# Scores in three steps of 512 columns, first half of O after four of h, and the gate spread by PE, in a kernel of attention and a sentence-level expert layer

## The chip, the cores and the metric

The kernel runs on one core of one Trainium2 chip. The metric is device microseconds of one execution. Every run of an experiment was timed beside runs of the kernel before on the same chip. A run is called fast or slow by its state; only fast runs are compared here.

An engine is named as the profile names it: PE is TensorE, PEld its weight loads, DVE VectorE, ACT ScalarE, POOL GpSimd, SP SyncE. A "quarter" is half a batch's heads: there are 8 batches and 16 quarters, each with four heads of 64 columns over a sequence of 576. The texts on record count quarters in two ways: "the quarter after the fourth" has index 4, counted from 0.

## The reference, cut to what matters

```python
# q, k, v: (8 batches, 8 heads, 576, 64); f: (8, 8, 576), gates in (0.8, 1)
scores = q @ k.T / 8
cum    = cumsum(log(clip(f, 1e-4, 1)))
scores = where(causal, scores + cum[i] - cum[j], -1e9)
attn   = softmax(scores)
x      = (attn @ v), heads side by side            # (8, 576, 512)
# one expert per batch
e      = argmax(x.mean(axis=1) @ w_gate)           # 8 experts
gate   = softmax(x.mean(axis=1) @ w_gate)[e]
out    = gate * (relu(x @ w1[e]) @ w2[e])          # w1: 512x1024, w2: 1024x512
```

The decay is folded into the weights of V, so that the device computes an exp of the plain scores, a mask, and two products: with weighted V, and with the weights alone for the row sums.

## The kernel before

The program is not written as a sequence. It declares some 1,090 operations with durations, dependences, buffers and priorities, and a list scheduler (class `Order`) plans them on a model of the engines and of the DMA queues. The plan is made when the kernel is built; what it leaves is one fixed order of instructions for each engine. On the chip each engine takes its instructions in that order and waits where an operand is missing.

```python
# constants of the scheduler that matter here
FILL = 60.0            # until then PE is given filler matmuls where its plan is empty
PM0  = 12.0            # priority of the expert layers against attention
LAG  = 3               # K and Q of a quarter are loaded three quarters ahead
LOOK = {1: (0, 0, 0), 2: (0, 1, 2), 3: (1, 0, 2), 4: (1, 0, 2)}   # quarters loaded early
...
# Order.run, cut: the free engine takes the ready operation of the lowest priority number
if pick is not None and (best is None or pick.prio < best[1].prio):
    best = (e, pick)
if best is None and self.filler is not None and now < self.fill_until and busy["PE"] <= now + 1e-9:
    ...                                     # a filler matmul: still (zeros), 128x512
```

Scores of a quarter take four steps of 448, 448, 384 and 320 columns; each step writes two PSUM tiles of two banks (two heads each), and each tile has an exp of its own:

```python
PS_S = [psum.tile([P, 2, 512], fp32, name=f"ps_s{i}") for i in range(2)]
...
def expo(g, s, halves):
    e = E[od.slot(("e", g))][s]
    for n in halves:
        nc.scalar.activation(e[:, 2 * n:2 * n + 2, :],
                             PS_S[od.slot(("s", (g, s, n)))][:, :, 0:WIDTH[s]], AF.Exp, scale=0.125)
...
raws[g, 1].behind = raws[g, 1].behind if g in LOOK else [ld2] if g < 6 else [wvs[g - LAG][0]]
```

The first two quarters go by half steps (two heads at a time). After a batch's two quarters come its gate, the load of its expert's weights, 64 matmuls of h (128x288, sixteen units of four) and ten units of O (the output product), which are planned side by side with the attention of later quarters.

The softmax here doesn't subtract the row's maximum and nothing guards it: scores larger than these inputs give would overflow.

Of the kernel before, what the change touches and what calls it, by code (L numbers as in the profile page):

```python
# [11 lines left out]
P = 128  # L12
S = 576
# [11 lines left out]
STEPS = (((0, 0, 448, 0),),  # L25
         ((1, 128, 576, 0),),
         ((2, 256, 576, 0), (4, 512, 576, 320)),
         ((3, 384, 576, 0), (0, 448, 576, 192)))
WIDTH = (448, 448, 384, 320)

BLOCKS = ((0, 256, ((0, 0, 0, 256, 0), (1, 1, 128, 256, 0))),
          (256, 576, ((1, 1, 256, 576, 128), (0, 0, 256, 448, 256), (2, 2, 256, 576, 0),
                      (0, 3, 448, 576, 192), (3, 3, 384, 576, 0), (4, 2, 512, 576, 320))))

MAX_SPAN = 72.0

W_LOW, W_HIGH = 8.6e-17, 1.2e16
LN_SCALE = 2.0 ** -3
FILL = 60.0
# [5 lines left out]
PM0 = 12.0  # L45
LAG = 3
# [5 lines left out]
LOOK = {1: (0, 0, 0), 2: (0, 1, 2), 3: (1, 0, 2), 4: (1, 0, 2)}  # L52


class Op:
# [3 lines left out]
    def __init__(self, name, engines, us, fn, after=(), prio=0.0, takes=(), gives=(), lands=None, grain=None, runs=0, behind=()):  # L59
        self.name, self.us, self.fn, self.prio = name, us, fn, prio  # L60
        self.engines = engines if isinstance(engines, tuple) else (engines,)
        self.after, self.takes, self.gives, self.lands = list(after), takes, gives, lands
        self.end, self.grain, self.runs = None, grain, runs
        self.behind, self.issued = behind, None
        self.engine = None


class Order:
# [4 lines left out]
    def __init__(self, rings):  # L73
        self.free = {k: [(0.0, i) for i in range(n)] for k, n in rings.items()}
        self.held = {}
        self.turn = {k: [] for k in rings if k != "bank"}
        self.ops = []
        self.queues = {"SP": [], "ACT": [], "POOL": []}
        self.clock, self.last = 0.0, "full"
        self.filler, self.fill_until, self.spare = None, 0.0, 0  # L80
# [22 lines left out]
    def advance(self, now):  # L103


        while self.clock < now - 1e-9:
# [9 lines left out]
            for q in live:  # L116
                if q[0][1] < 1e-6:
                    op = q.pop(0)[3]
                    op.end = self.clock + 0.4
                    self.give(op)  # L120

# [17 lines left out]

    def run(self):  # L140
        left = list(self.ops)
        busy = dict.fromkeys(("PE", "ACT", "DVE", "POOL", "SP"), 0.0)
        now = 0.0
        busy["PE"] = 2.0
        while left:
# [5 lines left out]
            for e, until in busy.items():  # L151
# [4 lines left out]
                for op in left:  # L156
                    if e not in op.engines:
                        continue
                    ready = 0.0
                    for a in op.after:  # L160
                        if a.end is None:
                            ready = None
                            break
                        ready = max(ready, a.end + (0.0 if a.engine == e and a.lands is None else self.HOP))
                    for a in op.behind:
                        if a.issued is None:
                            ready = None
                        elif ready is not None:
                            ready = max(ready, a.issued)
                    if ready is None:  # L170
                        continue
# [13 lines left out]
            if best is None and self.filler is not None and now < self.fill_until and busy["PE"] <= now + 1e-9:  # L185
# [9 lines left out]
            if best is None:  # L195
                assert horizon is not None, (self.held, [o.name for o in left if all(a.end is not None for a in o.after)])
# [3 lines left out]
            op.engine = e  # L200
            for ring, key in op.takes:
# [4 lines left out]
                if ring in self.turn:  # L206
                    self.turn[ring].pop(0)
            if e == "PE" and self.mode(op) != self.last:
# [11 lines left out]
            left.remove(op)  # L220
# [5 lines left out]
def fast_path(ctx, tc, q, k, v, f, moe_w_gate, moe_w1, moe_w2, out, flag):  # L226
# [12 lines left out]
    PS_S = [psum.tile([P, 2, 512], fp32, name=f"ps_s{i}") for i in range(2)]  # L239
# [3 lines left out]
    KT = [const.tile([P, S], fp32, name=f"kt{i}") for i in range(RINGS["qt"])]  # L243
    VF = [const.tile([P, NCH, NH, D], fp32, name=f"vf{i}") for i in range(RINGS["vf"])]
    VB = [const.tile([P, NCH, 4, D], bf16, name=f"vb{i}") for i in range(RINGS["vb"])]
    E = [[const.tile([P, 4, WIDTH[s]], bf16, name=f"e{s}{i}") for s in range(4)] for i in range(RINGS["e"])]
# [13 lines left out]
    ROW = small("row", [1, P])  # L260
    seen_to = const.tile([P, 1], fp32, name="seen")[64:65, :]
# [5 lines left out]
    span = const.tile([NB * NH, 1], fp32, name="span")  # L267
    mxs = const.tile([1, NB * NH], fp32, name="mxs")
    mx8 = const.tile([1, 8], fp32, name="mx8f")
    WF = const.tile([P, NB, NCH, NH], fp32, name="WF")  # L270
    WB = const.tile([P, NB, NCH, NH], bf16, name="WB")
    wg = const.tile([P, 4, NE], fp32, name="wg")
    ident = const.tile([D, D], fp32, name="identf")
    still = const.tile([P, 512], bf16, name="still")

# [34 lines left out]
    def first(op):  # L310
        nc.scalar.preload_act_table_set("natural_log_exp_and_others")
        nc.sync.dma_start(F, f.rearrange("b h s -> (b h) s"))
        nc.vector.memset(still, 0.0)  # L313
        for t in VB:
            nc.vector.memset(t[0:64, 4, :, :], 0.0)
        nc.vector.memset(WF[0:64, :, 4, :], 0.0)

    loadf = od.add("F", "SP", 0.5, first, prio=-50, lands=0.5, grain=.1)
    idop = od.add("ident", "POOL", 0.8, lambda op: make_identity(nc, ident), prio=-1)
# [9 lines left out]
    last = [loadf]  # L329
    for b in range(NB):  # L330
        for c in range(10 if b < VQ else 5):
# [3 lines left out]
                                   takes=(("vf", b),) if c == 0 else (), lands=(1.4 if c5 < 4 else .7) / (2 if b < VQ else 1), grain=.022, runs=(64 if c5 < 4 else 32) // (2 if b < VQ else 1),  # L335
                                   behind=last if b < VQ else [loads_v[b, c - 1]] if c else [])
# [13 lines left out]
    def cum3(op):  # L350
        nc.vector.tensor_scalar_mul(mid, span, -0.5)
        nc.vector.tensor_tensor_scan(CUM, LOGF, LOGF, mid[:, 0:1], op0=ALU.add, op1=ALU.bypass)
# [13 lines left out]
    def cum6(op):  # L366
        pw = PS_W[od.slot(("bank", "cum"))]
        for w in (WF[:, :, 0:4, :], WF[64:P, :, 4, :]):
            nc.vector.tensor_scalar(w, w, W_LOW, W_HIGH, op0=ALU.max, op1=ALU.min)
        nc.vector.tensor_copy(WB.rearrange("p b c h -> p (b c h)"), WF.rearrange("p b c h -> p (b c h)"))  # L370
# [5 lines left out]
    c2 = od.add("cum2", "ACT", 0.68, cum2, after=[c1], prio=0.5)  # L376
    c3 = od.add("cum3", "DVE", 1.45, cum3, after=[c2], prio=2)
    c4 = od.add("cum4", "PE", 0.8, cum4, after=[c3, idop], prio=0, takes=(("bank", "cum"),))
    c5 = od.add("cum5", "ACT", .7, cum5, after=[c4], prio=0)
    c6 = od.add("cum6", "DVE", 0.9, cum6, after=[c5], prio=0, gives=(("bank", "cum"),))  # L380
# [3 lines left out]
    def to_t(g, j, lo=0, hi=4):  # L384
        raw = RAW[j][od.slot(("raw", g))][32 * lo:32 * hi].bitcast(fp32).rearrange("p (r w) -> p r w", w=32)
        dst = (QT, KT)[j][od.slot(("qt", g))][32 * lo:32 * hi].rearrange("p (t r) -> p r t", r=18)
        nc.vector.transpose(dst, raw)  # L387

    def banks_of(g, s, n):

        i = od.slot(("s", (g, s, n)))
        return [(2 * n + j, PS_S[i][:, j, :]) for j in range(2)]

    def step(g, s, halves):
        i = od.slot(("qt", g))
        kt, qt = KT[i].bitcast(bf16).rearrange("p (t r) -> p t r", r=2), QT[i].bitcast(bf16).rearrange("p (t r) -> p t r", r=2)
        for c, i0, i1, col in STEPS[s]:
            for r in range(2):
                for h, ps in [x for n in halves for x in banks_of(g, s, n)]:
                    nc.tensor.matmul(ps[:, col:col + i1 - i0], kt[32 * h:32 * h + 32, KLO[c]:KLO[c] + P, r],  # L400
                                     qt[32 * h:32 * h + 32, i0:i1, r], start=(r == 0), stop=(r == 1))

    def expo(g, s, halves):
        e = E[od.slot(("e", g))][s]
        for n in halves:
            nc.scalar.activation(e[:, 2 * n:2 * n + 2, :], PS_S[od.slot(("s", (g, s, n)))][:, :, 0:WIDTH[s]], AF.Exp, scale=0.125)  # L406

    def mask(g, s):
        e = E[od.slot(("e", g))][s]
        nc.gpsimd.affine_select(out=e[:, :, 0:128], in_=e[:, :, 0:128], pattern=[[0, 4], [1, 128]],  # L410
                                channel_multiplier=-1, base=0, compare_op=ALU.is_ge, fill=0.0)
        if s == 2:
            nc.gpsimd.affine_select(out=e[:, :, 320:384], in_=e[:, :, 320:384], pattern=[[0, 4], [1, 64]],
                                    channel_multiplier=-1, base=64, compare_op=ALU.is_ge, fill=0.0)

    def weigh(op, g, part):
# [8 lines left out]
        else:  # L425
            eng.tensor_tensor(vb[64:P, 4, :, :], vf[64:P, 4, h, :],
                                    WF[64:P, b, 4, h].unsqueeze(2).to_broadcast([64, 4, D]), op=ALU.mult)

    def pv(g, blk, what, lo_n=0, hi_n=6):
# [38 lines left out]
    last_s = []  # L468
    tk, steps, exps, masks, pvs, wvs = {}, {}, {}, {}, {}, {}
    for g in range(NQ):  # L470
        b, m = divmod(g, 2)
        p = 3.0 * g
        for n in (0, 1) if g == 0 else ():
            for j in (1, 0):
                tk[0, j, n] = od.add(f"T0{j}h{n}", "DVE", 1.15, lambda op, j=j, n=n: to_t(0, j, 2 * n, 2 * n + 2), after=[raws[0, j, n]] + ([tk[0, 1, n]] if j == 0 else []), prio=p + .1 * n,
                                     takes=(("qt", 0),) if j > n else (), gives=(("raw", 0),) if n > j else ())
        for j in (1, 0) if g else ():
            tk[g, j] = od.add(f"T{g}{j}", "DVE", 1.15, lambda op, g=g, j=j: to_t(g, j), after=[raws[g, j]] + ([tk[g, 1]] if j == 0 else []), prio=p,
                              takes=(("qt", g),) if j == 1 else (), gives=(("raw", g),) if j == 0 else ())
        if g == 0:  # L480
# [3 lines left out]
        for part in (0, 1, 2):  # L484
            wv.append(od.add(f"V{g}{part}", "POOL" if g > 1 or part == 1 and g == 0 else "DVE" if g == 0 else ("DVE", "POOL"), 1.1 if part < 2 else 0.7, lambda op, g=g, part=part: weigh(op, g, part), prio=p + 1.5,
# [3 lines left out]
        for s in range(4):  # L489
            steps[g, s], exps[g, s] = [], []  # L490
        turns = [(s, x) for x in cut for s in range(4)] if g == 0 and len(cut) > 1 else [(s, x) for s in range(4) for x in cut]
        for s, halves in turns:
            n = WIDTH[s]
# [365 lines left out]
```

## Time and profile before

| | kernel before |
|---|---|
| median of three runs | 249.45 us (249.1 to 251.54) |
| profiled run, span | 250.8 us |
| first h matmul, last matmul ends | 39.3 us, 244.4 us |
| PE idle between them (gaps of 0.15 us or more, summed from the trace) | 8.7 us |

The prediction shows the page's first lines, a table of stages and three lines of the start. One more view is needed later: the table of PE's waits (columns: the waiting engine with what it writes and its line, the engine that released it with what it had written, then us in total, times, longest us).

```profile
PE ps_s L400 <- ACT e L406: 2.8, 6, 1.0
PE ps_w L595 <- DVE xT L459: 1.9, 1, 1.9
PE ps_w L439 <- issue: 1.5, 2, 0.9
PE ps_w L595 <- DMA w1e<-in_moe_w_dram: 1.5, 2, 1.0
```

The reader is to see that no wait is large: scores wait 2.8 us for exps in 250 us, and weights cost 1.5 us, all at the first expert. "Issue" means that the profile shows no releaser; what stands behind it turns up below.

### The profile page before, as it was taken

The page shows a single profiled execution, that of the slowest core. Times are in us where ns is not written, and L with a number is a line of the kernel's source. Part 1 is how long each engine was busy: PE and PEld are TensorE (multiplying, and loading weights), DVE is VectorE, ACT ScalarE, POOL GpSimd, SP SyncE. Part 2 cuts the span into 40 slices and gives each one's busy share as a digit, 9 for nine tenths or more (in the row PEclk, how much of TensorE's full clock was granted, in tenths as well). Part 3 has the DMA queues.
Part 4 walks back from the last instruction along what each step waited for, and adds up shares of the span by engine and source line. Part 5 has one row for each costly group of instructions (what it writes and reads, how often), then busy time and mean ns, then how long its engine had stood idle before and what let it go on. Part 6 is the DMA issues. An engine that isn't in the chain of part 4 may idle for free.

```text
span 250.8 us, 8039 instructions
## 1 busy us (share of the span) xinstructions
PE 229.7 (92%) x3304; PEld 146.2 (58%) x3325; DVE 115.4 (46%) x305; ACT 177.2 (71%) x313; POOL 127.0 (51%) x197
## 2 busy tenths in 40 slices
PE   6799997999889999799999999899998999999990
PEld 2333734674366846567458755586586656957840
DVE  3892882667533941278136942694146342200000
ACT  3466846897799968849779874896488787855820
POOL 6046739971995546714992649363822872300000
PEclk9657999999999999979999999999999999999996
DMA  6996849999999999990999999999993598299032
GB/s 119 221 221 118 146 73 180 201 207 212 177 220 212 215 204 226 297 213 8 173 219 213 277 218 215 254 227 209 227 278 76 82 232 216 36 212 256 29 121 75
DMA packets 59946, 45.84 MB, mean 183 GB/s; under 512 B 40896, under 2 KB 43968, under 8 KB 59904
## 3 DMA queue, kind: packets, MB, share of 16 engines
q0 software_dynamic: 14848, 26.22, 59.1%
q1 hardware_dynamic: 32576, 15.90, 25.1%
q10 hardware_dynamic: 12480, 3.15, 6.1%
q8 instruction: 28, 0.46, 0.7%
q14 instruction: 14, 0.11, 0.1%
HBM read 62.03 MB, written 9.44 MB: 285 GB/s over the span
## 4 chain that ended last, share of the span: by engine, by line
PE 73%; DMA 7%; issue 6%; POOL 6%; ACT 3%; DVE 2%; POOLq 1%; ACTq 0%; DVEq 0%
PE ps_w L595 24%; PE ps_w L612 20%; PE ps_s L400 12%; PE ps_w L439 11%; PE ps_w L615 3%; PE ps_w L680 3%; DMA out_dram<-otile 3%; DMA w1e<-in_moe_w_dram 2%; ACT e L406 2%; DMA rawq<-in_q_dram 2%; POOL e L410 2%; POOL vb L423 1%; DVE qt L387 1%; POOL rawk L281 1%; PE ps_w L548 1%
## 5 line engine op out<-in xcount | busy, mean ns | idle before, releaser
L406 ACT ACTIVATE e<-ps_s 128x896 bf16<-128x896 f32 (+2 forms) x128 | 100.2, 834 | 28.7 <-PE ps_s L400 27.9
L410 POOL TENSOR_SCALAR_AFFINE_SELECT e<-e 128x512 bf16<-128x512 bf16 x64 | 41.7, 656 | 69.0 <-ACT e L406 68.4
L595 PE MATMUL ps_w<-xT,w1e 128*128 128x288 bf16 x512 | 71.0, 292 | 3.4 <-DVE xT L459 1.9
L595 PEld LDWEIGHTS <-w1e 128*128 128x128 bf16 x512 | 60.5, 139 | 11.5 <-issue 4.9
L612 PE MATMUL ps_w<-w2e,h1T 128*128 128x512 bf16 x239 | 57.5, 380 | 1.9 <-issue 1.4
L400 PE MATMUL ps_s<-qt,kt 32*128 32x448 bf16 (+4 forms) x768 | 42.1, 289 | 5.6 <-ACT e L406 2.8
L459 DVE SCALAR_TENSOR_TENSOR xT<-ps_w,lr 128x256 bf16<-128x256 f32 (+1 forms) x64 | 26.8, 455 | 37.1 <-ACT lr L449 30.6
L605 ACT ACTIVATE h1T<-ps_w,gate_b 128x288 bf16<-128x288 f32 x77 | 37.4, 499 | 4.9 <-PE ps_w L595 4.7
L612 PEld LDWEIGHTS <-h1T 128*128 128x128 bf16 x256 | 22.8, 98 | 28.5 <-issue 3.6
L603 DVE TENSOR_SCALAR h1T<-ps_w,gate_b 128x288 bf16<-128x288 f32 x51 | 25.3, 505 | 28.6 <-PE ps_w L595 28.2
L400 PEld LDWEIGHTS <-kt 32*128 32x128 bf16 x768 | 17.6, 95 | 27.5 <-issue 21.5
L439 PE MATMUL ps_w<-e,vb 128*32 128x320 bf16 (+4 forms) x1024 | 29.4, 251 | 1.8 <-issue 1.5
L423 POOL TENSOR_TENSOR vb<-vf,WF 128x512 bf16<-128x512 f32 x29 | 30.5, 1053 | 0.3
L387 DVE STREAM_TRANSPOSE kt<-rawk 128x576 f32<-128x576 f32 (+1 forms) x17 | 21.3, 1252 | 19.4 <-DMA rawk<-in_k_dram 16.3
L624 ACT COPY otile<-ps_w 128x512 f32<-128x512 f32 (+1 forms) x25 | 14.0, 560 | 21.9 <-PE ps_w L612 20.9
L439 PEld LDWEIGHTS <-vb 128*32 128x32 bf16 x1024 | 21.3, 97 | 7.0 <-issue 4.7
L387 DVE STREAM_TRANSPOSE qt<-rawq 128x576 f32<-128x576 f32 (+1 forms) x17 | 21.1, 1244 | 0.6 <-DMA rawq<-in_q_dram 0.5
L680 PE MATMUL ps_w<-still 128*128 128x512 bf16 x51 | 17.4, 472 | 2.1 <-DVE still L313 1.4
L622 DVE COPY otile<-ps_w 128x512 f32<-128x512 f32 (+1 forms) x15 | 9.0, 599 | 21.2 <-PE ps_w L612 19.8
L439 PE MATMUL ps_w<-e,WB 128*32 128x192 bf16 (+4 forms) x512 | 17.3, 253 | 0.1
L576 POOL DMA_DIRECT2D w1e<-in_moe_w_dram x14 | 10.2, 731 | 13.1 <-DVE h1T L603 11.4
L444 ACT ACTIVATE lr<-ps_w 128x256 f32<-128x256 f32 (+1 forms) x31 | 12.7, 411 | 4.8 <-PE ps_w L439 4.5
(55 smaller groups left out, 129.4 us busy)
## 6 DMA issues: line engine op xcount, KB each, us to landing
w2e<-in_moe_w_dram POOLq DMA_DIRECT2D x8, 1024.0 KB, 14.2
out_dram<-otile SPq DMA_DIRECT2D x32, 256.0 KB, 7.4
w1e<-in_moe_w_dram POOLq DMA_DIRECT2D x14, 512.0 KB, 7.6
rawk<-in_k_dram POOLq DMA_DIRECT2D x15, 288.0 KB, 7.2
rawq<-in_q_dram POOLq DMA_DIRECT2D x15, 288.0 KB, 8.7
vf<-in_v_dram SPq DMA_DIRECT2D x12, 256.0 KB, 9.3
vf<-in_v_dram ACTq DMA_DIRECT2D x12, 256.0 KB, 12.2
vf<-in_v_dram SPq DMA_DIRECT2D x22, 128.0 KB, 6.0
```

The costliest lines, as they stand in the source:

```text
L387: nc.vector.transpose(dst, raw)
L400: nc.tensor.matmul(ps[:, col:col + i1 - i0], kt[32 * h:32 * h + 32, KLO[c]:KLO[c] + P, r], qt[32 * h:32 * h + 32, i0:i1, r], start=(r == 0 ...
L406: nc.scalar.activation(e[:, 2 * n:2 * n + 2, :], PS_S[od.slot(("s", (g, s, n)))][:, :, 0:WIDTH[s]], AF.Exp, scale=0.125)
L410: nc.gpsimd.affine_select(out=e[:, :, 0:128], in_=e[:, :, 0:128], pattern=[[0, 4], [1, 128]], channel_multiplier=-1, base=0, compare_op=AL ...
L423: eng.tensor_tensor(vb[:, c, :, :], vf[:, c, h, :], WF[:, b, c, h].unsqueeze(3).to_broadcast([P, 2, 4, D]), op=ALU.mult)
L439: nc.tensor.matmul(ps[32 * h:32 * h + 32, lo - i0:hi - i0], lhs, e[s][:, h, col:col + hi - lo], start=(n == 0), stop=(n == len(parts) - 1) ...
L459: nc.vector.scalar_tensor_tensor(XT[od.slot(("x", b))][:, mm, i0:i1], ps[:, 0:i1 - i0], 1.0 if (g, blk) in ON_DVE else LN_SCALE, LR[od.slo ...
L595: nc.tensor.matmul(ps[:, 0:288], lhs, xT[:, m, 288 * half:288 * half + 288], start=(m == 0), stop=(m == 3))
L603: nc.vector.tensor_scalar(dst, ps[:, 0:288], g[:, 0:1], 0.0, op0=ALU.mult, op1=ALU.max)
L605: nc.scalar.activation(dst, ps[:, 0:288], AF.Relu, scale=g[:, 0:1])
L612: nc.tensor.matmul(ps, h[:, j, P * sb:P * sb + P], r, start=(j == 0), stop=(j == 7))
L680: od.filler = lambda i: nc.tensor.matmul(PS_W[i], still[:, 0:P], still[:, 0:512])
```

## The change

It repacks the causal scores of a quarter into three steps of 512 columns, so that a whole step of four heads fills one PSUM tile of four banks exactly and gets one exp of 128x2048. Two pieces of 64 columns share a place by a K that is padded with zeros. It also lets the first half of an O product start after four of the eight h blocks, spreads the gate value over partitions by a PE matmul instead of a DMA, moves some masks to DVE, replaces clamps, lets V loads start only after f has landed, drops the fillers of the first 28 us of the plan, corrects durations in the scheduler's model, and changes its load constants. Its core:

```diff
-STEPS = (((0, 0, 448, 0),),
-         ((1, 128, 576, 0),),
-         ((2, 256, 576, 0), (4, 512, 576, 320)),
-         ((3, 384, 576, 0), (0, 448, 576, 192)))
+STEPS = (((0, 0, 512, 0),),
+         ((1, 128, 576, 0), (0, 512, 576, 448)),
+         ((2, 256, 576, 0), (None, 384, 512, 320), (3, 448, 576, 384)))
...
-FILL = 60.0
+FILL = (28.0, 60.0)
-PM0 = 12.0
-LAG = 3
+PM0 = 11.0
+LAG = 2
-LOOK = {1: (0, 0, 0), 2: (0, 1, 2), 3: (1, 0, 2), 4: (1, 0, 2)}
+LOOK = {1: (0, 0, 0), 2: (0, 1, 2), 3: (1, 0, 2)}
...
-    PS_S = [psum.tile([P, 2, 512], fp32, name=f"ps_s{i}") for i in range(2)]
+    PS_S = psum.tile([P, 4, 512], fp32, name="ps_s")
...
     def expo(g, s, halves):
         e = E[od.slot(("e", g))][s]
-        for n in halves:
-            nc.scalar.activation(e[:, 2 * n:2 * n + 2, :], PS_S[...][:, :, 0:WIDTH[s]], AF.Exp, scale=0.125)
+        if len(halves) == 2:
+            nc.scalar.activation(e, PS_S, AF.Exp, scale=0.125)
+        else:
+            for lo, bank in banks_of(g, s, halves):
+                nc.scalar.activation(e[:, lo:lo + 2, :], PS_S[:, bank:bank + 2, :], AF.Exp, scale=0.125)
...
     def gate6(op, b):
-        nc.sync.dma_start(GATE[i], ROW[i])
+        nc.tensor.matmul(ps[:, 0:1], ROW[i], one)
...
-            om = od.add(f"O{b}{sb}a", ..., after=list(rel.values()) + outs[-1:] + [ld2], ...)
+            om = od.add(f"O{b}{sb}a", ..., after=[x for (j, _), x in rel.items() if j < 4] + outs[-1:] + [ld2], ...)
```

One thing about it is easily read past: because the order is made by the scheduler, every changed duration and constant draws a new order for all engines, over the whole 250 us.

## The prediction

> **What bounds the kernel now.** I read the page first: busy shares, then the forty slices, then the chain of waits.
>
> ```profile
> span 250.8 us, 8039 instructions
> PE 229.7 (92%) x3304; PEld 146.2 (58%) x3325; DVE 115.4 (46%) x305; ACT 177.2 (71%) x313; POOL 127.0 (51%) x197
> ...
> PEclk9657999999999999979999999999999999999996
> ...
> PE 73%; DMA 7%; issue 6%; POOL 6%; ACT 3%; DVE 2%; POOLq 1%; ACTq 0%; DVEq 0%
> ```
>
> PE is busy 92% of the time and carries 73% of the chain, so an engine other than PE matters only where PE waits for it or runs filler. The clock row shows half clock in the first slices. The table of stages (columns: stretch, length, busy us of each engine with instruction counts, clock, DMA share, GB/s) separates a start, a body and a tail:
>
> ```profile
> 7.80:21.40 13.60, 13.03 (x74) 4.54 (x74) 11.27 (x17) 6.97 (x10) 5.19 (x8) 0.50 1.04 194
> 21.40:43.80 22.40, 19.89 (x342) 10.89 (x337) 13.13 (x33) 15.67 (x26) 14.78 (x26) 1.00 0.83 135
> 43.80:213.00 169.20, 161.67 (x2663) 106.67 (x2678) 85.06 (x238) 132.58 (x234) 100.48 (x149) 0.99 1.01 204
> 213.00:244.50 31.50, 31.11 (x225) 22.64 (x225) 2.46 (x13) 19.33 (x40) 2.19 (x3) 1.00 0.58 129
> ```
>
> Up to 43.8 us PE looks busy, but much of it is filler on the tile `still`: 51 matmuls, 17.4 us. By starts and columns, useful columns there are worth only about 15 us at full clock. The body and tail are nearly solid. The timeline shows what filler does in the start:
>
> ```profile
> 15.13 1.24 DVE L387 STREAM_TRANSPOSE qt<-rawq 128x576 f32<-128x576 f32 x1
> ...
> 18.64 2.31 PE L680 MATMUL ps_w<-still 128*128 128x512 bf16 x5
> ...
> 20.88 0.82 PE L400 MATMUL ps_s<-qt,kt 32*128 32x448 bf16 x8
> ```
>
> Queries of the second quarter are ready at 16.37 us, yet its first scores start at 20.88: PE takes instructions in their fixed order, and five fillers at half clock stand ahead of them. The same happens at 12.73 (three fillers ahead of scores whose operands were ready at 11.82). The exps of that quarter end at 29.3, its last normalization at 32.3, the gate follows, the first expert weights are issued at 35.48, and the first h matmul starts at 39.31. From there PE is the bound until 244.5; a copy and a store take the last 6.3 us.
>
> **What the Trainium skill says.** "TensorE: Matmul & The Clock Gate", Part 1, gives a clock that is half when cold and full after about 3.4 us of sustained work. The trace agrees on the two values: 0.5 from 7.79 to 21.44 us, 1.0 after, and one dip of 3.41 us at 106.8. Its Part 3 says that matmuls in different row groups run concurrently, starting about 4 ns apart; here four heads' matmuls start 3 to 4 ns apart. "TensorEngine Tiling (Array Packing)", Key Properties, says that changing the tiling mode drains the engine. The trace agrees: a warm 512-column matmul is followed by the next after 216 ns, but by a row-tiled score after 312, so a change costs about 96 to 110 ns. "ScalarE: Activation LUTs", Step-by-step: what each stage is for, gives 0.833 ns per element for an activation; here 896 columns take 913 ns and 768 take 807, that is 0.83 per column.
>
> **The change part by part.**
>
> *Scores.* Columns per head and quarter: before 2×(448+448+384+320) = 3200; after 2×(512+512+320+128) plus four shared pieces of 64 = 3200 again. Score matmuls go from 768 to 896, those of attention times values from 1536 to 1728. These are small ones, four side by side: groups of four of 64 columns start some 20 to 27 ns after one another, 128 columns 46, 192 columns 72. Columns decide, so PE pays nearly nothing.
>
> *Exps.* Before, by shape: 55.2+24.4+20.9 = 100.5 us. After: 42 of 128×2048 at an estimated 0.913+1152×0.00083 = 1.87 us, and 12 of 128×1024 at 1.02: 91 us. ACT gets some 10 us back. It was at 71%, so this is mostly off the path, but 12 exps stand on the path in the start.
>
> *Mode changes.* The built order has 168 changes of PE mode before and 133 after; from the first h matmul on, 140 and 118. 22 × 0.1 = **2.2 us** on the path.
>
> *Fillers.* 55 fall to 10, all after the first 28 us of the scheduler's plan. Also, loads of V now wait until f has landed, so Q and K come first. I walk the start. Before, the first Q half lands at 6.71, slowed by V loads from 1.61 on; after, I expect about 5.3, and first scores at 7.0 instead of 8.04. DVE then does its transposes some 1.1 us earlier; clamps (0.52) and the flag (0.6) leave its front; the second quarter's Q is ready near 14.7 instead of 16.37. With no filler ahead, its scores run from about 16 to 23, still at half clock (a pair of 512-column half steps is 4×512/1.2 GHz = 1.7 us). Its exps then end at 23.5 to 24.5 instead of 29.3. Masks and values add 2.5, exps of the row sums and normalization 1.1: last normalization at about 28 instead of 32.3. A 1.25 us transpose of Q that now stands between the pooled sums and the top logit moves ahead. Weights issued at about 30.1 instead of 35.48, first h at about 33.9: **5.4 us** earlier, with the same work done (3.0 quarters of scores against 2.83, two of values in both).
>
> *Gate by PE.* The spread by DMA took 6.3 us to land in the median, but h matmuls do not read it; in batch 1 it lands at 69.2 and h starts at 73.7. Hidden: 0. The eight new matmuls cost 1 us at most.
>
> *O after four of h.* In the tail before, the first O matmul follows the last h matmul 96 ns later, a plain mode change. Already not a wait on chip; it only loosens the planned order. About 0.
>
> *Body gaps.* Between 43.8 and 213 I add starts less columns over 2.4 GHz: about 10 us remain that are neither mode changes nor records missing from the trace. Scores waiting for exps are 3.5 of them; one wait is 2.0, at 104.5, where DVE stood on a late K load, and the clock dip after it costs 1.7 more. New durations in the scheduler (h copies 0.5 instead of 0.46, O copies 0.66 instead of 0.62) fit the trace better (0.50; 0.585 to 0.69), so I choose **4 us** regained of 12, with wide error.
>
> Sum: 5.4+2.2+4−1 = 10.6 off 249.45 gives 238.9; I take 238 since the ACT relief may give a little.
>
> **The rivals.** *Exps become a wait.* One exp now reads all four banks, so no score can start for about 2 us, where the two half exps let the first two heads go after 0.92. Where only 16 h matmuls (2.1 us) stand between two score steps, PE can wait a few tenths. There are 42 such steps; at 0.3 us on half of them this takes back 6 us and gives 244. Against it: scores already filled both halves in turn, and the wait on exps was only 2.8 us in total. *DMA bounds.* In the body its share is 1.01 and K loads land up to 14 us after issue. If transfers rather than PE set the pace, starting early wins nothing, and the time would be 246 to 249. Against: of all PE waits in the table only 1.5 us name a DMA, all at the first weights; 71.5 MB in 238 us is 300 GB/s against 285 now. *A cold start.* Without filler PE may stay at half clock past 25 us: scores and values of quarter 1 then take 2 to 3 us longer, giving 241. *The opposite*: all 12 us of body gaps vanish and exps in the start run back to back: 230.
>
> **Range and chances.** The start (2 to 8 us) and the body (−4 to +9) dominate. I put 8 in 10 on 231.5 to 245. Faster by 2% means below 244.5; only the exp or DMA rival in full prevents that: 0.86 faster, 0.12 within, 0.02 slower.
>
> **What would show it.** Right: first second-quarter score near 16 us, first h at 32 to 36, `still` at ten matmuls; exps of 2048 columns at about 1.87 us; 118 mode changes at 0.1; PE over 95% from first h to its end. Wrong: scores waiting for exps for more than 6 us in total, DVE standing on K loads, h waiting for weights again and again, or a first h after 38 us.

## The result, and the profile after

| | before | after |
|---|---|---|
| median, same session | 250.5 us (249.1 to 252.13, 4 runs) | 260.72 us (260.41 to 262.24, 4 runs) |
| profiled run, span | 250.8 us | 259.4 us |
| first h matmul | 39.3 us | 38.8 us |
| from first h to the end of the last matmul | 205.1 us | 214.7 us |
| PE idle in that stretch | 8.7 us | 16.7 us |
| end of the last matmul to the end | 6.4 us | 5.9 us |

The changed kernel is slower. Its ratio to the kernel before is 1.042 (95% interval 1.033 to 1.051). Ratios here are the mean time of one kernel's fast runs over the mean of the other's fast runs of the same rounds, so they are not quite the ratio of the medians quoted. The profiled runs of both are fast. That of the kernel before is at the slow end of its runs (252.5 us), that of the changed kernel near its median (260.93), so the profiles lie closer together (8.6 us) than the medians (10.2).

The 8.6 us between the two profiled spans fall into three parts of the table: −0.5 in the start, +9.6 in the body, −0.5 in the tail. Of the 9.6 in the body 8.0 are PE's idle time.

The page of the changed kernel, first its span and busy times, then the clock row and the chain by engine:

```profile
span 259.4 us, 8569 instructions
PE 220.2 (85%) x3597; PEld 147.5 (57%) x3616; DVE 137.0 (53%) x359; ACT 165.8 (64%) x231; POOL 122.4 (47%) x189
...
PEclk9999999997999999999999997999999999999999
PE 58%; DMA 19%; issue 8%; ACT 7%; DVE 3%; POOL 2%; POOLq 1%; SPq 0%; ACTq 0%
```

PE is busy 9.5 us less, though the useful work is the same, since most fillers are gone; but it carries 58% of the chain instead of 73%, and DMA 19% instead of 7%. The chain now runs through many waits. The table of stages, with the stretches laid at the same events (first score, clock full, body, the last 31.5 us of PE):

```profile
7.30:29.90 22.60, 16.40 (x258) 9.73 (x258) 15.87 (x27) 13.20 (x17) 10.54 (x18) 1.00 0.82 153
29.90:43.80 13.90, 10.60 (x192) 6.08 (x187) 9.95 (x31) 9.50 (x11) 9.74 (x16) 1.00 0.79 117
43.80:222.00 178.20, 162.00 (x2937) 109.03 (x2950) 98.02 (x261) 126.96 (x173) 95.83 (x140) 0.98 0.98 198
222.00:253.50 31.50, 31.18 (x224) 22.53 (x224) 8.30 (x24) 13.53 (x28) 2.21 (x3) 1.00 0.56 129
```

The tail is as it was, 31.2 us busy of 31.5. The body has 162.0 us of PE in 178.2 (91%), where before it was 161.7 in 169.2 (96%): the same work, in a longer time. In the start PE stands for 6.2 of 22.6 us. The clock of 1.00 in the first row is no measurement: the first record of the clock in this trace is at 29.9 us. Eight score matmuls of 512 columns took 1.05 us at 19.63 and 0.63 at 32.37, so PE was at half clock there.

What it stands for in the start shows in the timeline of PE (columns: start, us, engine, line, operation, out<-in, shape, count; in brackets the idle time before and its releaser):

```profile
7.30 1.89 PE L456 MATMUL ps_s<-qt,kt 32*128 32x512 bf16 x12 [7.30 <-DVE mid L391]
...
11.21 0.71 PE L456 MATMUL ps_s<-qt,kt 32*128 32x320 bf16 x4 [1.20 <-ACT e L464]
...
13.46 1.89 PE L456 MATMUL ps_s<-qt,kt 32*128 32x512 bf16 x12 [1.11 <-ACT e L464]
17.38 0.71 PE L456 MATMUL ps_s<-qt,kt 32*128 32x320 bf16 x4 [2.02 <-ACT e L464]
...
19.63 1.05 PE L456 MATMUL ps_s<-qt,kt 32*128 32x512 bf16 x8
```

The first score comes at 7.30, as predicted to 0.3 us. Then scores wait for exps three times, and the second quarter's first scores come at 19.63 instead of the predicted 16. The table of PE's waits says the same in sums:

```profile
PE ps_s L456 <- ACT e L464: 6.2, 5, 2.0
PE ps_s L456 <- ACT e L461: 5.3, 6, 2.0
PE ps_w L691 <- DMA w1e<-in_moe_w_dram: 3.6, 2, 2.5
PE ps_w L691 <- DVE xT L520: 2.7, 2, 1.9
PE ps_w L500 <- issue: 2.1, 1, 2.1
```

Line 464 is the half exps of the first two quarters, line 461 the whole ones. Scores now wait 11.5 us for exps, against 2.8. The weights cost 3.6 us, 2.5 of them once, at batch 4. And the exps themselves, in the table of groups by form (name, shapes, count; busy us and mean ns; idle before):

```profile
L461 ACT ACTIVATE e<-ps_s 128x2048 bf16<-128x2048 f32 x42 | 78.7, 1875 | 18.6 <-PE ps_s L456 16.4 <-DMA out_dram<-otile 1.4
L464 ACT ACTIVATE e<-ps_s 128x1024 bf16<-128x1024 f32 x12 | 11.7, 1021 | 11.6 <-PE ps_s L456 11.6
```

They take 90.4 us, where the prediction had 91. Relief of ACT is real, but ACT's share of the chain rose from 3% to 7%: scores wait for single exps, whatever the sum.

Where the time goes over the run was read by marking when the same share of useful PE columns is done in both kernels. Up to 55 us of useful work in 172 the changed kernel is behind by up to 6 us (batch 0: the fourth K is issued at 42.0 us and lands at 57.5, DVE stands on it, and h waits 1.9 us behind DVE). By 140 us it has caught up to within 0.2 us. Between 152 and 166 us it loses 7 us at one blow and never gets them back: the gate of batch 4 comes at 150.3 us instead of 135.7, the expert layer of batch 3 is used up, so scores follow one another with nothing between, wait for exps, and then h waits for the weights of batch 4.

### The profile page after: what moved, and what is told of

It reads as the page before. It is cut to its first block, busy times and chain, and to the rows that moved or that the text cites. A ratio compares the mean times of both kernels' runs of the same rounds, so it can differ in the third digit from the quotient of the medians.

```text
span 259.4 us, 8569 instructions
## 1 busy us (share of the span) xinstructions
PE 220.2 (85%) x3597; PEld 147.5 (57%) x3616; DVE 137.0 (53%) x359; ACT 165.8 (64%) x231; POOL 122.4 (47%) x189
## 4 chain that ended last, share of the span: by engine, by line
PE 58%; DMA 19%; issue 8%; ACT 7%; DVE 3%; POOL 2%; POOLq 1%; SPq 0%; ACTq 0%
PE ps_w L691 20%; PE ps_w L708 17%; PE ps_s L456 9%; DMA vf<-in_v_dram 7%; PE ps_w L500 7%; DMA rawk<-in_k_dram 6%; DMA w1e<-in_moe_w_dram 4%; ACT e L464 4%; PE ps_w L711 3%; ACT e L461 2%; DMA rawq<-in_q_dram 1%; POOL w1e L661 1%; DVE qt L431 1%; DVE xT L520 1%; PE ps_w L617 1%
## 5 line engine op out<-in xcount | busy, mean ns | idle before, releaser
L461 ACT ACTIVATE e<-ps_s 128x2048 bf16<-128x2048 f32 x42 | 78.7, 1875 | 18.6 <-PE ps_s L456 16.4
L691 PEld LDWEIGHTS <-w1e 128*128 128x128 bf16 x512 | 60.1, 139 | 14.8 <-issue 7.2
L456 PE MATMUL ps_s<-qt,kt 32*128 32x512 bf16 (+4 forms) x640 | 38.4, 314 | 19.3 <-DVE mid L391 7.3
L701 ACT ACTIVATE h1T<-ps_w,gate_b 128x288 bf16<-128x288 f32 x71 | 35.1, 499 | 26.9 <-PE ps_w L691 23.8
L472 POOL TENSOR_SCALAR_AFFINE_SELECT e<-e 128x512 bf16<-128x512 bf16 x43 | 28.5, 663 | 49.0 <-ACT e L461 37.8
L699 DVE TENSOR_SCALAR h1T<-ps_w,gate_b 128x288 bf16<-128x288 f32 x57 | 28.7, 513 | 31.8 <-PE ps_w L691 31.0
L456 PEld LDWEIGHTS <-kt 32*128 32x128 bf16 x640 | 15.2, 97 | 36.0 <-issue 25.9
L500 PE MATMUL ps_w<-e,vb 128*32 128x64 bf16 (+3 forms) x1152 | 31.4, 251 | 1.3 <-ACT lr L505 1.2
L500 PE MATMUL ps_w<-e,WB 128*32 128x64 bf16 (+3 forms) x576 | 18.8, 257 | 2.4 <-issue 2.1
L470 DVE TENSOR_TENSOR e<-e,causal 128x512 bf16<-128x512 bf16 x20 | 13.1, 661 | 14.0 <-ACT e L461 11.3
L647 POOL DMA_DIRECT2D w1e<-in_moe_w_dram x14 | 10.2, 731 | 20.2 <-DVE h1T L699 14.0
L464 ACT ACTIVATE e<-ps_s 128x1024 bf16<-128x1024 f32 x12 | 11.7, 1021 | 11.6 <-PE ps_s L456 11.6
```

Of the source, the lines that this page charges most:

```text
L456: nc.tensor.matmul(ps[:, col:col + i1 - i0], kt[row, KLO[c]:KLO[c] + P, r], qt[row, i0:i1, r], start=(r == 0), stop=(r == 1))
L461: nc.scalar.activation(e, PS_S, AF.Exp, scale=0.125)
L464: nc.scalar.activation(e[:, lo:lo + 2, :], PS_S[:, bank:bank + 2, :], AF.Exp, scale=0.125)
L472: nc.gpsimd.affine_select(out=x, in_=x, pattern=[[0, 4], [1, P]], channel_multiplier=-1, base=0, compare_op=ALU.is_ge, fill=0.0)
L500: nc.tensor.matmul(ps[32 * h:32 * h + 32, lo - i0:hi - i0], lhs, e[s][:, h, col:col + hi - lo], start=(n == 0), stop=(n == len(parts) - 1) ...
L691: nc.tensor.matmul(ps[:, 0:288], lhs, xT[:, m, 288 * half:288 * half + 288], start=(m == 0), stop=(m == 3))
```

## The experiments

Seventeen kernels ran, in five sessions. They are told in the order in which they ran, by what they tell apart.

### One part undone: score tiles, the fourth K, the fillers, the weights

**e1: two score tiles again.** The static order is the same as in the changed kernel.

```diff
-    PS_S = psum.tile([P, 4, 512], fp32, name="ps_s")
+    PS_S = [psum.tile([P, 2, 512], fp32, name=f"ps_s{i}") for i in range(2)]
...
-        if len(halves) == 2:
-            nc.scalar.activation(e, PS_S, AF.Exp, scale=0.125)
-        else: ...
+        for lo, bank in banks_of(g, s, halves):
+            nc.scalar.activation(e[:, lo:lo + 2, :], PS_S[bank // 2], AF.Exp, scale=0.125)
```

> The changed kernel with one thing undone: the scores go into two tiles of two banks again, and a step of 512 columns has two exps of 128x1024 instead of one of 128x2048. The static order is the same. Theory A (the single tile makes each exp wait for both heads' pairs, and the next scores for the whole exp): PE's waits for the exps in scores fall from 11.5 us (6.2 + 5.3) to below 4, the first h matmul comes at 34 to 36 us instead of 38.79, and the time is 253 to 257. Theory B (the clock stays at half until 29.9 us, so the start is paced by PE): first h moves by less than 1 us and the time stays within 1 us of 260. Theory C (late loads set the pace of the whole): first h is earlier but the time stays at 259 to 261, since h of batch 0 still waits for the late fourth K.

Measured: 259.73 us, 1.037 of before (1.031 to 1.043). The timeline of PE in the start:

```profile
10.14 0.71 PE L456 MATMUL ps_s<-qt,kt 32*128 32x320 bf16 x4
...
17.01 1.05 PE L456 MATMUL ps_s<-qt,kt 32*128 32x512 bf16 x8 [0.82 <-DVE qt L431]
```

The waits for exps are gone from the start (3.7 us remain in the whole run), the second quarter starts at 17.01, and the first h comes at 34.8 us, 4.0 us earlier: theory A holds for the start, and theory B (clock) falls, since nothing was done for the clock. The time did not follow: about 1 us of it is left. In its profile, which is the fastest of its four runs, the kernel is some 4 us ahead of the kernel before at 140 to 148 us, loses 8 us in the next 15, and ends 5.4 us behind.

**e2: the fourth K early.** The order of every engine is kept; only two loads move.

```diff
+        early = [log[at[n]] for n in ("raw41", "raw40")]      # K and Q of quarter 4
+        log = rest[:n] + early + rest[n:]                     # n: right behind those of quarter 3
```

> The changed kernel with the order of every engine kept, except that the K and Q loads of the quarter after the fourth one are issued right behind those of the fourth, ahead of the first expert weights (in the kernel before they stood there too). Theory C (a K load issued at 42.0 and landed at 57.5, on which DVE stood for 3.5 us, holds up h of batch 0): DVE's wait at 57 us goes, the last h of batch 0 starts at 55 to 57 us instead of 61.3; if this is never given back the time is 255 to 257. Theory D (it is given back, since around 80 to 95 us the changed kernel had caught up with the kernel before): the time stays at 259 to 261.

Measured: 260.44 us, 1.039 (1.034 to 1.044). DVE's wait for that K is gone, but the two loads that moved forward push the first weights back: they land at 40.7 us instead of 38.5, and PE stands for them.

```profile
40.74 0.42 PE L704 MATMUL ps_w<-xT,w1e 128*128 128x288 bf16 x2 [1.57 <-DMA w1e<-in_moe_w_dram]
```

So the first h comes at 40.74 instead of 38.79, and the last h of batch 0 at 62.0 instead of 61.3, with new waits of 1.3 us for h1T and 1.4 us of "issue" on the way. The time is that of theory D, but the move paid for what it took away. From the first h to the end of the last matmul e2 takes 212.0 us against 214.7, so that late load was not free; this place for it gains nothing.

**e3: fillers back where PE waited in the start**, in the kept order.

```diff
+        plan = {"S02h0": 2, "S01h1": 2, "S02h1": 4, "S11h0": 2, "S11h1": 2, "S12h0": 2, "S20": 1}
+        # that many filler matmuls ahead of each of these scores
```

> The changed kernel with its order kept and 15 filler matmuls put back where PE waited before scores in the start (2, 2, 4, 2, 2, 2 and 1). Theory B (half clock for want of work): the groups of 512-column scores fall from 1.05 us per eight to 0.63 before 20 us, and the first h comes 2 to 4 us earlier, time 256 to 258. Theory A (waits for the exps set the pace): first h moves by less than 1 us, and the time stays at 259 to 261.

Measured: 266.64 us, 1.061 (1.054 to 1.068); first h at 43.8 us, 5 us later. Both theories miss, and the sign is what teaches:

```profile
10.34 1.03 PE L794 MATMUL ps_w<-still 128*128 128x512 bf16 x2
...
16.75 1.89 PE L794 MATMUL ps_w<-still 128*128 128x512 bf16 x4
```

At half clock a filler takes 0.43 us, and PE takes it in order even where the operand behind it is there. The clock did come up earlier (eight score matmuls of 512 columns take 0.64 us at 20.65, which is full clock, against 1.05 at 19.63 without fillers), and it did not pay. Nor did it last: by the clock's records it was full from 18.62 to 25.45 us, and half again until 32.28.

**e4: no expert weights after batch 2** (wrong on purpose; relative error 1.1).

```diff
     def weights1(op, b, a):
+        ...
+        if b >= 3:
+            return                     # the loads of batches 3 to 7 are left out
```

> The changed kernel without the loads of expert weights for batches 3 to 7 (they compute with the weights of earlier ones: wrong on purpose). It moves some 20 MB less through the DMA. Theory E (transfers bound the whole body): V and K land early, the time falls below 248. Theory F (the slip at 145 to 165 us is the wait for the weights of batch 4, landed 12 us after the gate): that part goes alone, and the time is 252 to 256. Theory G (the order of the instructions, with scores waiting for exps, is the whole cause): the time is 258 to 261.

Measured: 259.14 us, 1.032 (1.027 to 1.037). Theory E, that transfers bound the body, is out, with the prediction's second rival: 21 MB less to read (41.1 against 62.0 MB) gain about 1%. Theory F is nearly out too: the loss of 7 us at that place is still 6.4 us, with no weights to wait for; PE waits for exps 0.7 and 2.0 us there instead, and runs at half clock behind these waits. Of the three theories G, the order, remains; that is a conclusion by exclusion.

### The load plan, and the tile alone

**e5: two tiles, and the load constants of before.**

```diff
-LAG = 2
-LOOK = {1: (0, 0, 0), 2: (0, 1, 2), 3: (1, 0, 2)}
+LAG = 3
+LOOK = {1: (0, 0, 0), 2: (0, 1, 2), 3: (1, 0, 2), 4: (1, 0, 2)}
     # and PS_S as in e1; one dependence more (the last V piece of quarter 3 behind the V of quarter 2),
     # without which the build fails; e12, e15 and e16 have it too
```

> The changed kernel with two score tiles and, besides, the load plan of the kernel before (K and Q loads let go three scores ahead instead of two, and the quarter after the fourth in the early list). The scheduler then makes another order. Theory H (the thinner load plan made the order bad: K of batch 5 issued at 133 us instead of 102, the gate of batch 4 at 150 instead of 136, so attention and the expert layers no longer lie side by side there): the gate of batch 4 comes before 141 us, the stretch of 8 us lost between 150 and 166 us goes, and the time is 245 to 250. Theory G' (any order of this scheduler runs some 12 us behind its plan because its durations are too short): the time is 255 to 260.

Measured: 256.96 us, 1.023 (1.013 to 1.032). The gate of batch 4 comes at 139.8 us and the loss between 150 and 166 us is gone, as theory H says, but the time is above its range: other losses stand elsewhere (5 us between 39 and 57, 4.6 us between 91 and 102). The time lies in the range of theory G', that any order of this scheduler runs some 12 us behind its plan; it comes up again below.

**e6: the kernel before with the load constants of the change.**

```diff
-LAG = 3
-LOOK = {1: (0, 0, 0), 2: (0, 1, 2), 3: (1, 0, 2), 4: (1, 0, 2)}
+LAG = 2
+LOOK = {1: (0, 0, 0), 2: (0, 1, 2), 3: (1, 0, 2)}
```

> The kernel before with one part of the change alone: the thinner load plan (two scores ahead instead of three, no early entry for the quarter after the fourth). Theory H (the load plan costs the time): 254 to 259. Rival (loads had 3 to 10 us of slack in the kernel before, so nothing comes of it): 250 to 252.

Measured: 264.41 us, 1.055 (1.045 to 1.065). Two lines cost the kernel before 13 us, more than the whole change does. In its trace seven of the twelve K loads from quarter 4 to 15 land just as DVE takes them (slack 0.0 us); in the kernel before, three do.

**e7: the kernel before, two score tiles declared as one.** Order kept, nothing else changed.

```diff
-    PS_S = [psum.tile([P, 2, 512], fp32, name=f"ps_s{i}") for i in range(2)]
+    PS_S = psum.tile([P, 4, 512], fp32, name="ps_s")
```

> The kernel before, its order kept, with its two score tiles declared as one tile of four banks, and nothing else changed; its exps stay half as wide as those of the changed kernel. Theory A (one tile makes exps wait for scores of the other pair of heads, and scores for exps of the other pair): PE's waits for exps rise from 2.8 us to more than 7, and the first h comes 1 to 4 us later than 39.3; time 253 to 257. Rival (the width of the exps and not the tile makes those waits): time within 1 us of 251.

Measured: 255.55 us, 1.018 (1.010 to 1.026). Waits of scores for exps rise from 2.8 to 8.2 us and the first h comes at 41.9 us, 2.6 later.

```profile
PE ps_s L400 <- ACT e L406: 8.2, 13, 1.8
```

So one tile is enough to make such waits, without a wider exp: the program's dependences are kept per tile, and scores of one half wait for the exp of the other half.

**e8: the kernel before without its early fillers**, order kept.

```diff
-    od.filler = lambda i: nc.tensor.matmul(PS_W[i], still[:, 0:P], still[:, 0:512])
+    od.filler = lambda i: od.clock >= 28.0 and nc.tensor.matmul(PS_W[i], still[:, 0:P], still[:, 0:512])
```

> The kernel before, its order kept, with the filler matmuls of the first 28 us of its plan left out and nothing put in their place. The prediction's step (fillers at half clock stood ahead of scores whose operands were ready): first scores of the second quarter before 18 us instead of 20.88, first h at 35 to 37 instead of 39.31, time 247 to 249. Rival (without fillers the clock stays at half and the start loses what it gained): first h at 38.5 to 40, time 250 to 252. Second rival (the gain is real in the start and given back in the body, where other waits set the pace): first h at 35 to 37, but time 250 to 252.

Measured: 251.3 us, 0.999 (0.989 to 1.010). The first h comes at 36.6 us, 2.7 earlier, and the last matmul of the profiled run ends 2.2 us earlier; in the timed runs that is within the interval (1% is 2.5 us). The prediction's claim that fillers delay the start is right; what that is worth in time this run cannot tell.

### Late loads, or the order that came with them

**e9: e1, with all K and Q loads from quarter 4 on issued where the kernel before's rule would put them** (quarter 5 keeps its place); compute order kept.

```diff
+        put = {"raw30": 4, **{f"V{g - 3}0": g for g in range(6, NQ)}}   # load g right behind this
```

> The changed kernel with two score tiles (as in e1) and the order of every compute instruction kept; only the K and Q loads of all quarters from the fourth on are issued earlier, where the rule of the kernel before (three scores ahead) would put them. Theory H1 (the late landing of K is what costs): time 2.5% or more below that of e1 (259.7), so 250 to 253. Theory H2 (the order in which PE, ACT and POOL take their work, which the scheduler made from the thinner load plan, is what costs; the loads themselves do not): within 1.5 us of e1, 258 to 261.

Measured: 260.89 us, 1.042 (1.037 to 1.047). K now lands 4 to 36 us ahead of its use. In e1 DVE stood on K loads for 6.6 us:

```profile
DVE kt L431 <- DMA rawk<-in_k_dram: 6.6, 5, 3.2
```

In e9 that row is gone from the table of DVE's waits, and in its place PE's table has

```profile
PE ps_w L715 <- DMA w1e<-in_moe_w_dram: 6.0, 4, 2.5
```

where e1 had 3.6: the loads that moved forward push the weights back. Theory H2: with this order, the loads have no place that helps.

**e10: e6 with its loads moved the same way.**

> The kernel of e6 (before with the thinner load plan, 264.4) with the order of its compute instructions kept and only its K and Q loads issued earlier again, as in the kernel before. Theory H1 (late landing): 250 to 255. Theory H2 (the order that came with it): 262 to 266.

Measured: 260.16 us, 1.040 (1.035 to 1.045), against 1.055 of e6. It lies between the two ranges: by these two ratios, which come from different sessions, the landing is about 1.5 of e6's 5.5% and the order that came with it 4.0, each by about 1 either way.

**e11: the kernel before with only LAG = 2.**

> The kernel before with half of the load plan's change: two scores ahead instead of three, but the quarter after the fourth kept in the early list. Its scheduler plans an end 2.4 us before that of the kernel before. If the missing early entry made the loss of e6: 248 to 252. If the two scores ahead made it: 260 to 265.

Measured: 256.12 us over all four runs, two of them slow; the two fast ones give 1.012 (0.999 to 1.025). Inconclusive on its own: the missing early entry, or the order drawn with it, is the larger part of e6, but whether two ahead costs anything is open.

**e12: a candidate, two tiles, the early entry back, PM0 = 12.** Of all orders tried its plan ends earliest.

> A candidate: the changed kernel with two score tiles, two scores ahead, the quarter after the fourth back in the early list, and expert layers one step later in the scheduler's priority, for which it plans the earliest end of all orders tried (0.9 us before that of the changed kernel). If its plan holds as e1's does, but for the late fourth K (8 to 10 us later on the chip): 250 to 254. If orders of this scheduler differ by several us on the chip for reasons that its plan does not see: anywhere from 250 to 262, with no relation to the plan.

Measured: 257.54 us, 1.028 (1.021 to 1.034). (The median is over five runs, of which two, the profiled one too, are slow; the ratio is over the three fast ones.) The plan's promise does not hold.

### Structure or order

After e12 each part of the change had been undone and some 2% was left over. The question was whether the new structure costs it, or any newly drawn order does.

```diff
 e13: kernel before, -PM0 = 12.0   +PM0 = 11.0
 e14: kernel before, -LAG = 3      +LAG = 4
 e15: e5,            -PM0 = 11.0   +PM0 = 12.0
 e16: e5,            -LAG = 3      +LAG = 4,    -PM0 = 11.0   +PM0 = 10.0
```

> The kernel before with one scheduler constant changed that asks for no other work (expert layers one step earlier in the priority; its plan ends 0.1 us later than that of before). Order theory: 253 to 260, though nothing but the order differs. Structure theory: 249 to 252.

> The kernel before with K and Q loads let go four scores ahead instead of three, which its plan puts 1.8 us ahead. Order theory: 253 to 260. Structure theory: 248 to 252, better than before if earlier loads help.

> The changed kernel with two score tiles and the load plan of before (e5), but expert layers one step later in the priority; its plan ends 0.6 us before that of e5. Order theory: anywhere from 251 to 260, on average as e13 and e14. Structure theory: 255 to 260.

> The changed kernel with two score tiles, loads four scores ahead, the early entry of the fourth quarter, and expert layers one step earlier; its plan ends 1.3 us after that of e5. Order theory: anywhere from 251 to 260. Structure theory: 255 to 260.

Measured: e13 260.38 us (one slow run of five, the profiled one), e14 253.46, e15 256.39, e16 262.92. With the earlier runs there are now four other orders of the old structure and five of the new one with two tiles. The plan's end is the end of the last matmul in the scheduler's own model, no time of a chip:

| structure | kernel | plan's end | ratio to before |
|---|---|---|---|
| before | before itself | 243.9 | 1 |
| before | e6 | 248.6 | 1.055 (1.045 to 1.065) |
| before | e11 | 241.5 | 1.012 (0.999 to 1.025) |
| before | e13 | 244.0 | 1.034 (1.029 to 1.040) |
| before | e14 | 242.1 | 1.006 (1.001 to 1.011) |
| changed, two tiles | e1 | 238.1 | 1.037 (1.031 to 1.043) |
| changed, two tiles | e5 | 238.4 | 1.023 (1.013 to 1.032) |
| changed, two tiles | e12 | 237.2 | 1.028 (1.021 to 1.034) |
| changed, two tiles | e15 | 237.8 | 1.020 (1.014 to 1.026) |
| changed, two tiles | e16 | 239.7 | 1.046 (1.040 to 1.052) |

The means of the two groups are 1.027 and 1.031. Their difference, 0.4%, is well inside the spread of the orders; with four and five orders it is known to some 2.4% either way (an estimate from the spread of the two groups), so a cost of the new structure is neither seen nor excluded. What is shown is that a redraw alone can cost nearly as much as the whole change: one constant that asks for no other work (e13) moves the old kernel by 3.4%. That the redraw is what cost it here is concluded by exclusion, and parts of the change that all the two-tile kernels keep were never undone alone: the masks on DVE (busy for 137.0 us instead of 115.4), the V loads behind f, the gate by PE, O after four. The order of the kernel before is the fast end of its own group. That is what one expects of a tuned kernel, whose constants were kept because their order ran well; that they were so chosen is argued here, not shown.

### A kept order with one wait taken out

**e17: the kernel before, every compute order kept, early fillers out (e8), and the K and Q loads of quarter 9 moved** right behind the weights of batch 2.

```diff
+        early = [log[at[n]] for n in ("raw91", "raw90")]
+        log = rest[:n] + early + rest[n:]        # n: right behind the load "w2" of batch 2
```

> The kernel before, every engine's order of compute kept, without the fillers of the first 28 us of the plan (as e8) and with the K and Q loads of the quarter after the ninth one issued right behind the second expert layer's weights of batch 2, some 14 us earlier. If idle PE time in the body turns into time: the wait of 2 us near 102 to 105 us and the clock dip behind it go, and with the 2 us of e8 the time is 247 to 249, 1 to 1.5% below before. If it is given back at the next wait: 250 to 252.

Measured: 247.64 us (245.34 to 248.31, 6 runs), 0.986 (0.981 to 0.991). It is faster than both kernels, by 1.4% against the kernel before, which is clear of noise though under the 2% that the record's verdict asks; the expectation holds in size. The table of stages over about the same stretch of work, first of the kernel before, then of e17 (columns as above, the last three clock, DMA share, GB/s):

```profile
97.00:114.00 17.00, 15.13 (x291) 11.49 (x291) 7.13 (x19) 11.70 (x22) 9.39 (x13) 0.90 1.04 236
```

```profile
95.00:112.00 17.00, 16.98 (x335) 13.56 (x332) 9.84 (x27) 14.87 (x28) 9.71 (x15) 1.00 1.14 243
```

The wait of 2 us is gone, and with it the half clock behind it (0.90 becomes 1.00; e17's trace has full clock from 23.49 to 245.36 us). Here idle time did become time. A kept order alone does not do that: e2 and e9 kept theirs and gained nothing, since their earlier loads pushed weights back, while here PE's waits for weights stay at 1.6 us against 1.5. The run holds two edits, and the moved load alone was not timed; e8's 0.999 (0.989 to 1.010) for the other one leaves its share between nothing and all.

## Why the prediction was wrong, point by point

- **The start, −5.4 us: the step that failed first.** Measured −0.5. Its walk assumed that half exps give back half of the score banks ("Scores already filled both halves in turn" is its words for the body). With one tile they do not: scores waited 6.2 us for the half exps. With two tiles (e1) the first h came at 34.8 against the predicted 33.9, so 4.5 of the 5.4 were right. A smaller miss lies in it: the second quarter's Q was ready at 17.2 us, not 14.7, because the loads of its K and Q were issued from 8.6 on instead of 5.5, behind a look at a V piece that itself now waited for f.
- **Body gaps, −4 us: the step that failed most.** Measured +8.0 of PE idle and +9.6 in all. It took better durations in the scheduler for fewer gaps. The plan did get shorter (238.1 against 243.9), but the chip ran 15.4 us behind that plan, where it ran 0.5 us behind the old one. Both plans, read by building the kernels again, put the first h 4.8 to 4.9 us too early; from there the chip took 4.4 us less than the old plan and 10.6 us more than the new one. And fewer gaps were hardly promised: planned PE idle after the first h is 17.0 us before and 15.6 after (8.7 and 16.7 on the chip), and most of the shorter plan is planned PE work that fell from 192.6 to 188.6 us, in part because durations were rewritten. A new order is a new draw, and e13 shows what a draw can cost by itself.
- **Mode changes, −2.2 us: right.** 120 are in the trace after the first h against 140 (118 had been predicted), and one costs 98 ns in the median in both traces, so it was 2.0 us. The spacing of small groups was read too low (64, 128 and 192 columns most often start 28, 56 and 82 ns apart in that trace, in the products with V), but columns decide, as it said: PE's busy time in the body is 161.7 and 162.0 us.
- **Exps, 91 us: right in size** (90.4). That they are mostly off the path was not: scores waited 11.5 us for them.
- **Fillers: right in count (10), and right that they delay** (e3, e8); **O after four and the gate by PE: about nothing**, as said; no run shows otherwise, and none tested them alone.
- **Rivals.** "Exps become a wait" was the one in force, but named for the body and priced at 6 us; it took 8.7 us more than before, 6.2 of them in the start. "DMA bounds" is refuted by e4. "A cold start" came true as a state: PE was at half clock until about 29.9 us. What it cost no run isolates; e3 shows only that these fillers cost more than they won. (The prediction's own table has PE busy, fillers included, for 13.03 of 13.60 us at half clock, so the 3.4 us of work that it took from the skill were not enough there.) Three signs named for a wrong prediction came: scores waiting for exps for more than 6 us, DVE on K loads, a first h after 38 us. The second tells nothing, since DVE waits longer for K in the faster kernel (first line before, second after; 16.3 and 5.9 us, 5 times each):

```profile
DVE kt L387 <- DMA rawk<-in_k_dram: 16.3, 5, 7.3
DVE kt L431 <- DMA rawk<-in_k_dram: 5.9, 5, 3.5
```

- **The range.** It gave the body −4 to +9 us of gain, so a loss of 4 at worst; a loss of 9.6 was not in it, since no view of one kernel's profile shows how good its order is among others. The chance for slower should not have been 0.02 for a change that redraws everything.

What stays open: which property makes one order good, and whether the new plans are too short for a reason of their own. In the profiled runs the last matmul ends 10 to 16 us behind the plan in all five two-tile orders, and 0.5 to 13 us in the five old ones (e11, e12 and e13 were profiled slow). Old structure with the new durations, which would part the two, was not run. Plans of 237 to 249 us give no ranking of the chip's times in the table, and no single kind of wait carries the difference: scores on exps, h on weights, DVE on K, PE on its instructions each take 1 to 4 us of it.

## What to carry to other kernels

Where a scheduler makes the order, measure a change in the kept order first, part by part, and draw new orders only in numbers, each timed; a single redraw of the old kernel here was worth from +0.6 to +5.5% with hardly any change in the work. Two uses of one tile are one dependence: before merging buffers so that an instruction can be wider, ask who could start early before. And a wait of 2 us on PE can cost more than its length: the one at 104.8 us was followed by 3.41 us of half clock, that is some 1.7 us more.

## What the Trainium skill lacked or had wrong

- "TensorE: Matmul & The Clock Gate", Why this matters for your kernels, advises against idle gaps of more than about 3 us, after which the clock halves. Shorter gaps were enough here (the page's Part 1 also tells of short idle spells that do it, without a length). In the kernel before an idle time of 1.86 us (104.8 to 106.7) was followed by half clock: its twelve h matmuls took 3.00 us, where twelve at 52.4 us take 1.65. In the changed kernel the same came after 1.88 us before 59.1 us: eight h matmuls took 1.65 us at 60.1, against 1.15 in e2. The first case, in the kernel before:

```profile
106.70 3.00 PE L595 MATMUL ps_w<-xT,w1e 128*128 128x288 bf16 x12 [1.86 <-DVE xT L459]
```

- "Trainium Architecture — The Big Picture", The software stack, has the instruction streams brought into each engine at load; "Runtime: NRT & Kernel Launch", Instruction fetch mechanics, corrects it: an engine goes on fetching its next instructions by DMA while it runs, which that page calls mostly hidden. The trace agrees on the fetching (the table of DMA queues has 30 instruction packets of 0.49 MB in the changed kernel), but hidden it may not always be. PE stood for 2.15 us in the middle of a group, with no semaphore to wait for:

```profile
48.77 0.28 PE L500 MATMUL ps_w<-e,WB 128*32 128x256 bf16 x4
51.21 0.24 PE L500 MATMUL ps_w<-e,WB 128*32 128x128 bf16 x4 [2.15 <-issue]
```

  An instruction packet landed 1.26 us before it went on. All 15 such stalls of over 0.3 us in five fast traces (before, after, e1, e5, e15) end 1.25 to 1.63 us after a packet has landed; that is read from the traces, and no experiment tested it. With the smaller ones they sum to 1.8 us in the kernel before, 2.5 in the changed one and 3.6 in e15. No page has a figure for such a stall, nor says that "issue" in such a table can stand for one.
